# Attention and dense layers in one kernel: row totals placed after the value step, their reciprocals spread by one matmul instead of two

## The chip, the cores and the metric

One core of a Trainium2 chip. Times are device microseconds (us) of whole executions, medians of fast runs (the record sorts executions into fast and slow ones; none here was slow); every profile shown is of state fast, with a granted TensorE clock of 0.998 to 1.0. TensorE is the matrix engine (PE in the profile, PEld its weight loads), DVE is VectorE, ACT ScalarE, POOL GpSimd.

## The reference, cut to what matters

```python
# 4 batches, 8 heads, 768 positions, 64 columns a head: 32 heads, worked on as 16 pairs
mask = q_bucket[:, :, :, None] == k_bucket[:, :, None, :]      # 6-bit hashes of q and k
scores = np.where(mask, scale * q @ k.T, -1e9)
attn = np.exp(scores - scores.max(-1, keepdims=True))
attn = attn / (np.sum(attn, axis=-1, keepdims=True) + 1e-09)   # needs the row totals
x = attn @ v                                                   # the value step
h = x.transpose(0, 2, 1, 3).reshape(3072, 512) @ w_in          # the dense layers
out = (np.maximum(h, 0) ** 2) @ w_out                          # weights come as float64
```

## The kernel before

Scores are kept transposed (keys on partitions), so a row total is a sum over partitions: DVE adds the exponentials of the six key blocks (`add_up`), a matmul with ones sums over the partitions (`sum_up`), and the reciprocals are brought to the layout of the value product (`spread`). The float64 weights are loaded and converted piece by piece beside the attention (`part_weight`, `round_weight`).

```python
def part_weight(i):                       # every third step
    nc.vector.tensor_scalar(out=power, in0=high, ...)          # L127
    nc.vector.tensor_scalar(out=top, in0=high, ...)            # L131
    nc.gpsimd.tensor_scalar(out=power, ...)                    # L136, then L139
    nc.scalar.activation(out=one, in_=top, func=ACTF.Copy, scale=2.0**-23, bias=1.0)   # L142
def round_weight(i):                      # one step later
    nc.vector.scalar_tensor_tensor(out=power, ...)             # L152
    nc.vector.scalar_tensor_tensor(out=one, ...)               # L156
    nc.gpsimd.tensor_tensor(out=pieces[i][3], in0=one, in1=power.bitcast(FP32), op=ALU.mult)
...
def score(pr, kt):                        # 8 matmuls (12 records) into two double banks, then 2 exponentials
    st = [ps_s.tile([P, 2, 512], FP32, name="st") for _ in range(2)]      # pool of two
    ...
def sum_up(pr):
    tot = bank("tot")
    ...                                   # 4 matmuls (8 records) tot <- ones, totals
    nc.vector.transpose(out=flip, in_=tot[:, 0:HS])
    nc.vector.tensor_scalar(out=once, in0=..., scalar1=S * TINY, ..., op0=ALU.add)
    nc.vector.reciprocal(out=once, in_=once)
    onces[pr] = once, tot
def spread(pr):
    once, tot = onces.pop(pr)
    rec = tot[:, HS:HS + 2 * NB]
    for c in range(2):
        nc.tensor.matmul(out=rec[:, c * NB:(c + 1) * NB], lhsT=picks[:, c], rhs=once, ...)
    nc.vector.transpose(out=recs[pr]..., in_=rec...)
...
for u in range(len(steps) + 2):           # 16 pairs x 6 steps
    add_up(*steps[u - 1]); score(*steps[u])
    done = steps[u - 2]
    if done[1] == SB - 1: spread(done[0])
    ...                                   # transposes or hash bits of the next pair
    if done[1] == SB - 2: sum_up(done[0])
    attend(*done)                         # the value block: 4 matmuls (8 records) xo <- v_nat, e
    if done[1] == SB - 1: normalize(done[0])
    i, r = divmod(u, 3)
    if r == 0: load_weight(i); part_weight(i - 1)
    if r == 1: round_weight(i - 1)
```

## Time and profile before

1076.4 us (median of 6 runs, 1075.9 to 1077.3). The dense layers begin at 408.6 us of the profile and are not touched. The attention part is read block by block: the start of one TensorE block to the start of the next, since ends of matmuls are modelled. "Third" and "sixth" count the score blocks of a pair from its first (key block 0). The pair length is the mean distance of spreads over 12 inner pairs.

| block, inner pairs | us |
|---|---|
| score block without a wait (third) | 1.72 |
| sixth score block | 2.10 |
| value block | 1.44 |
| totals | 1.16 |
| spread | 0.47 |
| whole pair | 24.49 |

### The profile page before, as it was taken

What the parts mean: (1) busy time and instruction counts of PE and PEld (TensorE: products, weight loads), DVE (VectorE), ACT (ScalarE), POOL (GpSimd) and SP (SyncE); (2) the same over time, 40 slices, a digit from 0 to 9 for tenths busy, and PEclk for the clock granted to TensorE, in tenths of its full rate; (3) what the DMA queues carried; (4) which work ended last, traced back from release to release, by engine and by line L of the source; (5) the groups of instructions that cost most, each with busy time, mean ns of one, the idle gap of its engine ahead of it and who ended that gap; (6) DMA issues with size and microseconds to landing.
All of it is one profiled execution on the core that took longest, in us unless ns stands there. A gap on an engine that the chain in (4) does not pass through costs nothing.

```text
span 1075.2 us, 10208 instructions
## 1 busy us (share of the span) xinstructions
PE 1055.7 (98%) x4098; PEld 460.4 (43%) x4098; DVE 424.2 (39%) x577; ACT 286.6 (27%) x457; POOL 116.1 (11%) x114
## 2 busy tenths in 40 slices
PE   6999999999999999999999999999999999999998
PEld 3444444444444434444444444444444444444443
DVE  2888888888888883200242024200210021002100
ACT  4555555555555541100110011101110011001100
POOL 1232323223223230000000000000000000000000
PEclk9999999999999999999999999999999999999999
DMA  8333333333331110000330033000000000000000
GB/s 200 84 84 84 84 85 84 84 90 121 107 101 55 40 40 1 0 10 20 127 117 10 20 122 109 15 18 20 1 0 20 20 1 0 20 20 1 0 20 21
DMA packets 65012, 55.24 MB, mean 51 GB/s; under 512 B 51648, under 2 KB 55744, under 8 KB 64960
## 3 DMA queue, kind: packets, MB, share of 16 engines
q1 hardware_dynamic: 63328, 54.14, 17.3%
q8 instruction: 34, 0.56, 0.2%
q10 hardware_dynamic: 1568, 0.39, 0.2%
q14 instruction: 18, 0.15, 0.0%
q0 software_dynamic: 64, 0.00, 0.0%
HBM read 48.24 MB, written 6.29 MB: 51 GB/s over the span
## 4 chain that ended last, share of the span: by engine, by line
PE 82%; DVE 9%; issue 6%; ACT 2%; DMA 0%; SPq 0%; ACTq 0%
PE hid L492 31%; PE y L509 31%; PE st L302 8%; PE xo L334 7%; DVE total L323 2%; PE tp L242 2%; ACT e L309 2%; PE tot L351 2%; DVE bits L266 2%; DVE x_t L384 1%; DVE one L156 1%; PE tot L370 1%; DVE power L152 1%; DVE power L127 1%; DMA q_nat<-in_q_dram 0%
## 5 line engine op out<-in xcount | busy, mean ns | idle before, releaser
L492 PE MATMUL hid<-x_t,w_in 128*128 128x512 f32 x768 | 330.8, 592 | 0.0
L509 PE MATMUL y<-w_out,gate 128*128 128x512 f32 x768 | 330.6, 592 | 0.0
L500 DVE TENSOR_TENSOR gate<-r 128x512 f32<-128x512 f32 x96 | 66.5, 693 | 508.8 <-ACT r L498 506.8
L509 PEld LDWEIGHTS y<-w_out,gate 128*128 128x128 f32 x768 | 145.9, 190 | 183.7 <-issue 183.4
L492 PEld LDWEIGHTS hid<-x_t,w_in 128*128 128x128 f32 x768 | 145.8, 190 | 183.3 <-issue 183.3
L309 ACT ACTIVATE e<-st 128x768 f32<-128x768 f32 x192 | 144.9, 806 | 108.8 <-PE st L302 108.8
L302 PE MATMUL st<-feat,feat 64*128 64x384 f32 x768 | 158.3, 485 | 0.0
L334 PE MATMUL xo<-e,v_nat 128*64 128x384 f32 (+1 forms) x768 | 146.4, 503 | 0.0
L323 DVE TENSOR_TENSOR total<-total,e 128x768 f32<-128x768 f32 x128 | 145.6, 1186 | 1.5 <-ACT e L309 1.5
L498 ACT ACTIVATE r<-hid 128x512 f32<-128x512 f32 x96 | 57.3, 597 | 277.0 <-PE hid L492 277.0
L514 ACT COPY o<-y 128x512 f32<-128x512 f32 x24 | 14.0, 585 | 315.8 <-PE y L509 315.8
L302 PEld LDWEIGHTS st<-feat,feat 64*128 64x128 f32 x768 | 69.3, 188 | 26.9 <-issue 26.4
L334 PEld LDWEIGHTS xo<-e,v_nat 128*64 128x64 f32 x768 | 46.8, 137 | 73.3 <-issue 73.2
L302 PE MATMUL st<-bits,bits 64*128 64x384 bf16 x384 | 70.7, 327 | 3.6 <-ACT e L309 1.5
L302 PEld LDWEIGHTS <-bits 64*128 64x128 bf16 x384 | 19.8, 93 | 69.9 <-issue 56.2
L323 DVE TENSOR_TENSOR total<-e,e 128x768 f32<-128x768 f32 x32 | 45.3, 1456 | 6.3 <-ACT e L309 6.3
L136 POOL TENSOR_SCALAR power<-power 128x512 uint32<-128x512 uint32 x32 | 22.9, 717 | 180.1 <-DVE power L127 180.1
L142 ACT ACTIVATE one<-one 128x512 f32<-128x512 uint32 x32 | 20.2, 630 | 73.3 <-DVE one L131 73.3
L159 POOL TENSOR_TENSOR w_in<-one,power 128x512 f32<-128x512 f32 x16 | 30.7, 1918 | 56.9 <-DVE one L156 56.9
L159 POOL TENSOR_TENSOR w_out<-one,power 128x512 f32<-128x512 f32 x16 | 30.0, 1876 | 55.9 <-DVE one L156 55.9
L247 ACT COPY feat<-tp 128x384 f32<-128x384 f32 x64 | 31.1, 486 | 5.1 <-PE tp L242 5.1
L139 POOL TENSOR_SCALAR power<-power 128x512 uint32<-128x512 uint32 x32 | 29.1, 910 | 2.6
(66 smaller groups left out, 384.1 us busy)
## 6 DMA issues: line engine op xcount, KB each, us to landing
raw<-in_moe_w_in_dram SPq DMA_DIRECT2D x16, 512.0 KB, 4.5
raw<-in_moe_w_out_dram SPq DMA_DIRECT2D x16, 512.0 KB, 4.0
q_nat<-in_q_dram SPq DMA_DIRECT2D x32, 192.0 KB, 5.1
v_nat<-in_v_dram SPq DMA_DIRECT2D x16, 384.0 KB, 3.4
out_dram<-o SPq DMA_DIRECT2D x24, 256.0 KB, 2.0
raw_qk<-in_q_dram SPq DMA_DIRECT2D x8, 768.0 KB, 4.4
raw_qk<-in_k_dram SPq DMA_DIRECT2D x8, 768.0 KB, 4.3
k_nat<-in_k_dram SPq DMA_DIRECT2D x30, 192.0 KB, 5.2
```

Of the source, the lines that this page charges most:

```text
L136: nc.gpsimd.tensor_scalar(out=power, in0=power, scalar1=1151.0, scalar2=896.0, op0=ALU.min, op1=ALU.max,)
L139: nc.gpsimd.tensor_scalar(out=power, in0=power, scalar1=-896.0, scalar2=2.0**23, op0=ALU.add, op1=ALU.mult,)
L159: nc.gpsimd.tensor_tensor(out=pieces[i][3], in0=one, in1=power.bitcast(FP32), op=ALU.mult)
L247: nc.scalar.copy(out=feat[pr, w][:, r * HS:(r + 1) * HS], in_=tp[:, 0:HS])
L302: nc.tensor.matmul(out=st[h][:, c, 0:HS], lhsT=src[pr, 1][rows, key], rhs=src[pr, 0][rows, cut], start=first, stop=not first,)
L309: nc.scalar.activation(out=e[:, 0:S].rearrange("p (c f) -> p c f", c=2), in_=st[h][:, :, 0:HS], func=ACTF.Exp, scale=scale,)
L323: nc.vector.tensor_tensor(out=totals[pr, h], in0=in0, in1=weights[pr, kt, h][:, 0:S], op=ALU.add)
L334: nc.tensor.matmul(out=xo[h * D:(h + 1) * D, c, 0:n], lhsT=nat[pr][2][:, h, kt * D:(kt + 1) * D], rhs=weights[pr, kt, h][:, c * HS:c * HS ...
L492: nc.tensor.matmul(out=hp, lhsT=w_in[:, ft, ff * P:(ff + 1) * P], rhs=x_t[:, ft, i * NCH:(i + 1) * NCH], start=(ft == 0), stop=(ft == NFT ...
L498: nc.scalar.activation(out=r, in_=hp, func=ACTF.Relu)
L500: nc.vector.tensor_tensor(out=g, in0=r, in1=r, op=ALU.mult)
L509: nc.tensor.matmul(out=y, lhsT=gates[ff][:, n * P:(n + 1) * P], rhs=w_out[:, ff], start=(ff == 0), stop=(ff == NFF - 1),)
```

## The change

Intent: the totals need DVE's last addition, so put the value block, which doesn't, ahead of them; and load one 128-column pattern instead of two, paying with a small product on DVE.

```diff
@@ -174,7 +174,8 @@
     lifts = const.tile([P, 1], FP32, name="lifts")
     pj = const.tile([P, NBITS], FP32, name="pj")
     ones = const.tile([P, 32], FP32, name="ones")
-    picks = const.tile([P, 2, P], FP32, name="picks")
+    picks = const.tile([P, P], FP32, name="picks")
+    which = const.tile([P, 2, HS // 32], FP32, name="which")
     NRING = 8
     ring = [const.tile([P, S + 1], FP32, name=f"e{i}") for i in range(NRING)]
 
@@ -204,11 +205,14 @@
 
 
         for g in range(4):
-            for c in range(2):
-                at = 64 * (g // 2) + 32 * c
-                nc.gpsimd.tensor_copy(
-                    out=picks[:, c, g * 32:(g + 1) * 32], in_=ident[:, at:at + 32]
-                )
+            cut = picks[:, g * 32:(g + 1) * 32]
+            at = 64 * (g // 2)
+            nc.gpsimd.tensor_tensor(
+                out=cut, in0=ident[:, at:at + 32], in1=ident[:, at + 32:at + 64], op=ALU.add
+            )
+        nc.gpsimd.memset(which, 0.0)
+        for g in range(4):
+            nc.gpsimd.memset(which[g * 32:(g + 1) * 32, g % 2], 1.0)
 
 
 
@@ -360,16 +364,20 @@
             scalar1=S * TINY, scalar2=None, op0=ALU.add,
         )
         nc.vector.reciprocal(out=once, in_=once)
-        onces[pr] = once, tot
+        both = p_n.tile([P, 2, NB], FP32, name="both")
+        nc.vector.tensor_tensor(
+            out=both, in0=which,
+            in1=once.rearrange("p (o n) -> p o n", o=1).to_broadcast([P, 2, NB]), op=ALU.mult,
+        )
+        onces[pr] = both, tot
 
     def spread(pr):
 
-        once, tot = onces.pop(pr)
+        both, tot = onces.pop(pr)
         rec = tot[:, HS:HS + 2 * NB]
-        for c in range(2):
-            nc.tensor.matmul(
-                out=rec[:, c * NB:(c + 1) * NB], lhsT=picks[:, c], rhs=once, start=True, stop=True
-            )
+        nc.tensor.matmul(
+            out=rec, lhsT=picks, rhs=both.rearrange("p c n -> p (c n)"), start=True, stop=True
+        )
         recs[pr] = p_n.tile([P, S], FP32, name="recs")
         nc.vector.transpose(
             out=recs[pr].rearrange("p (n f) -> p n f", f=32),
@@ -421,9 +429,9 @@
                 if pr + ahead < NP:
                     f(pr + ahead, *args)
             if done is not None:
+                attend(*done)
                 if done[1] == SB - 2:
                     sum_up(done[0])
-                attend(*done)
                 if done[1] == SB - 1:
                     normalize(done[0])
             i, r = divmod(u, EVERY)
```

## The prediction

> **What bounds the kernel now.** I read the page first, then the matrix engine's rows with shapes kept apart, then the timeline of all engines round the end of a head pair, then that of the last pair.
>
> ```profile
> PE 1055.7 (98%) x4098; PEld 460.4 (43%) x4098; DVE 424.2 (39%) x577; ACT 286.6 (27%) x457; POOL 116.1 (11%) x114
> L370 PE MATMUL tot<-once,picks 128*128 128x12 f32 x64 | 9.8, 264 | 0.0
> ```
>
> TensorE looks saturated from end to end. The two dense layers (from 408.59 us) are untouched and only shift. The change lies in the attention part, 16 pairs of 6 steps; a step is a score block (L302) on TensorE, its exponentials on ScalarE (ACT), additions on VectorE (DVE), and a value block (L334) two steps behind. Because matmul ends are modelled, short waits don't show as idle time: I measure from the start of one block to the start of the next. This is the hand-over from one pair to the next:
>
> ```profile
> 232.77 0.55 PE L242 MATMUL tp<-ident,q_nat 128*128 128x128 f32 x3
> 233.25 1.23 PE L351 MATMUL tot<-total,ones 128*32 128x384 f32 x8
> 234.41 1.51 PE L334 MATMUL xo<-e,v_nat 128*64 128x384 f32 x8
> 234.54 0.58 DVE L356 STREAM_TRANSPOSE flip<-tot 128x384 f32<-128x384 f32 x1 [0.96 <-PE tot L351]
> 235.16 0.17 DVE L358 TENSOR_SCALAR once<-flip 128x12 f32<-128x12 f32 x1
> 235.37 0.23 DVE L362 RECIPROCAL once<-once 128x12 f32<-128x12 f32 x1
> 235.51 0.45 DVE L127 TENSOR_SCALAR power<-raw 128x512 uint32<-128x512 uint32 x1
> 235.86 0.34 PE L302 MATMUL st<-bits,bits 64*128 64x384 bf16 x2
> 235.88 0.41 DVE L131 TENSOR_SCALAR one<-raw 128x512 uint32<-128x512 uint32 x1
> 236.38 0.63 ACT L142 ACTIVATE one<-one 128x512 f32<-128x512 uint32 x1 [1.57 <-DVE one L131]
> 237.57 0.61 PE L370 MATMUL tot<-once,picks 128*128 128x12 f32 x4
> 237.74 1.51 ACT L309 ACTIVATE e<-st 128x768 f32<-128x768 f32 x2 [0.72 <-PE st L302]
> 238.04 0.52 PE L242 MATMUL tp<-ident,k_nat 128*128 128x128 f32 x3
> 238.50 1.51 PE L334 MATMUL xo<-e,v_nat 128*64 128x384 f32 x8
> 239.94 0.34 PE L302 MATMUL st<-bits,bits 64*128 64x384 bf16 x2
> ```
>
> Block costs by differences of starts: totals 234.41-233.25 = 1.16, value block 235.86-234.41 = 1.45, score block 237.57-235.86 = 1.71, spread 238.04-237.57 = 0.47, transposes 0.46. In pair 0 the totals took only 0.89, and in pairs 1 to 13 always 1.16 or 1.17: so **0.27 us of each is a wait** for DVE's last addition. A pair lasts 24.49 us. A second wait hides in the last score block of each pair:
>
> ```profile
> 224.84 0.42 DVE L131 TENSOR_SCALAR one<-raw 128x512 uint32<-128x512 uint32 x1
> 225.35 0.63 ACT L142 ACTIVATE one<-one 128x512 f32<-128x512 uint32 x1 [2.86 <-DVE one L131]
> 225.88 1.49 ACT L309 ACTIVATE e<-st 128x768 f32<-128x768 f32 x2
> 227.03 0.71 PE L302 MATMUL st<-bits,bits 64*128 64x384 bf16 x2
> 229.13 0.55 PE L242 MATMUL tp<-ident,q_nat 128*128 128x128 f32 x3
> ```
>
> This block lasts 229.13-227.03 = 2.10 instead of 1.72. The weight conversion (L142) stands in ACT's queue ahead of the exponentials and gets its input late; the exponentials end at 227.37, and until then the second half of the score banks isn't free. **That costs 0.38 us per pair**, and DVE is its origin: from the normalisation on, DVE works without a gap up to L131.
>
> **What the Trainium skill says.** "TensorE: Matmul & The Clock Gate", LDWEIGHTS: loading weights takes columns/1.2 ns, so 107 ns for 128 columns. The trace agrees: spread is 4 matmul records (an fp32 matmul is two) at 0.47/4 = 0.117 us, though each moves only 12 columns. Same page, Architectural detail: ACT and DVE run strictly first in, first out; the L142 case above shows that on ACT. "VectorE: DVE Perf Modes", The TRN2 errata: an fp32 tensor_tensor takes (N+151)/0.96 ns; the 512-element gate product gives 691 and the page of the profile has 693. The clock page, Part 1: the array runs at half clock after an idle window of about 3.4 us; see the tail below.
>
> **The change part by part.** T is the start of the score block that follows the hand-over.
>
> 1. Totals after the value block: the matmuls are the same, but DVE's additions have 1.45 us more, so the wait of 0.27 goes. Saving 0.27 per pair.
> 2. Spread with one matmul: two weight loads instead of four, 0.47 to about 0.235. Twelve more columns add some 0.01 per record, by the score block's rate (feature matmuls of 384 columns, two side by side, take 0.32: four records in 0.65). Saving 0.23 per pair.
> 3. Added on DVE: one product of 128x24. Estimate from the skill's formula (24+151)/0.96 = 182 ns, and 35 ns between dependent instructions (235.16-234.54-0.58 = 0.04), so 0.22 us.
> 4. What moves: today the transpose starts 0.13 after the totals block ended, i.e. 1.32 before T. Afterwards the totals end at T, so it starts at T+0.13: the chain is **1.45 later against the score block**. In today's spacing: once +0.62, reciprocal +0.83, product +1.09, done +1.28, i.e. T+1.41. Spread comes at T+1.72: it just makes it, with 0.3 to spare.
> 5. The weight step follows on DVE: L131 at today's +1.34 after the transpose plus 0.22, so T+1.69 (today T+0.02). On ACT, L131's start to the end of both exponentials is 227.37-224.84 = 2.53 where the conversion leads. So exponentials end at T+4.22 instead of T+3.39. The next score block wants their banks at T + 1.72 + 0.235 + 0.46 + 1.44 = T+3.86. **A new wait of 0.36, with 0.04 to the restart 0.40 us**, in the third score block of the next pair.
> 6. The normalisation comes before this new wait, and DVE's unbroken work starts from it, so the older wait is measured from there too. TensorE arrives 0.40 later, and the old 0.38 vanishes. The two don't add: per pair the larger counts.
>
> Sum for an inner pair: -0.27 -0.23 +0.40 -0.38 = -0.48, times 13 = 6.2 us. The first hand-over has no wait to lose: -0.23+0.40-0.38 = -0.2. At the last but one the totals took 1.65, so -0.76-0.23 = -1.0; the new wait is harmless there, as the last pair hangs on DVE's additions.
>
> The tail:
>
> ```profile
> 401.88 2.23 PE L351 MATMUL tot<-total,ones 128*32 128x384 f32 x8 [1.94 <-DVE total L323]
> 404.04 2.63 PE L334 MATMUL xo<-e,v_nat 128*64 128x384 f32 x8
> ```
>
> Here TensorE idles 1.94, then runs the value block in 2.56 (404.04 to 406.60) instead of 1.44, a half clock. Afterwards this block runs inside that gap, at full clock; but after the totals TensorE must wait out the chain of 1.28 before spread, and may then be slow in the last value block. Dense layers start at 408.59 today; I estimate 406.6 if the clock holds, 408.5 if not: -1.0.
>
> Total 6.2+0.2+1.0+1.0 = 8.4: 1076.4-8.4 = 1068.0. I choose 1068.5, since step 5 is more likely to come out dearer than cheaper.
>
> **The rivals.**
> A. *No new wait*: ACT gets its conversion early enough. Then the old 0.38 stays and a pair takes 23.99, nearly the same as mine: about 1068. For it: a margin of 0.69 between the exponentials' end and the next score block today. Against it: the shift is 0.83.
> B. *The new wait is larger and eats the gain*: the product takes 0.4 instead of 0.22, or the exponentials come behind yet another ACT instruction. Each 0.1 us costs 1.5 us in all; a wait of 0.8 gives about 1074.5. For it: DVE additions beside GpSimd's products run at 1.45 instead of 0.93, so DVE durations do stretch here; against it: GpSimd is idle in this stretch.
> C. *Spread itself waits*: the margin of 0.3 is lost, TensorE stops in order. Beyond it each 0.1 again costs 1.5 us; 1070 to 1073. Against it: nothing stands between transpose and product on DVE.
> D. *Nothing lost at all*: both waits gone, 0.88 per pair, 1062. Against it: the queue order of ACT.
>
> **Range and chances.** Mine and A fall together at 1067 to 1069; B and C spread upward, the tail is worth 1 either way. Range 1065.5 to 1072.5. A result beyond 2% would need 1.35 us per pair, which no part carries: faster 0.01, same 0.98, slower 0.01.
>
> **What would show it.** Totals at 0.89 each; spread at 0.23 to 0.25 with 32 records instead of 64; the product near 0.18; the conversion L142 starting about T+2.2; the third score block of a pair (the one after the transposes and value block that follow spread) at about 2.1 instead of 1.72, and the sixth back at 1.72; pair length near 24.0. I am wrong if the pair takes over 24.3 (B or C, told apart by which block is long) or under 23.8 (D).

## The result, and the profile after

The changed kernel takes **1066.93 us** (median of 6, 1065.64 to 1067.32) against 1076.38; the ratio is 0.991, interval 0.9897 to 0.9923. (A ratio here is the mean time of one kernel's fast runs over that of the other's of the same rounds, so not quite the ratio of the medians.) This is faster by 0.9%, so within the 2% called the same, and inside the predicted range.

The timeline of all engines at the same hand-over, after:

```profile
231.57 0.85 PE L355 MATMUL tot<-total,ones 128*32 128x384 f32 x8
232.36 0.34 PE L306 MATMUL st<-bits,bits 64*128 64x384 bf16 x2
232.49 0.58 DVE L360 STREAM_TRANSPOSE flip<-tot 128x384 f32<-128x384 f32 x1 [2.03 <-PE tot L355]
...
233.58 0.18 DVE L368 TENSOR_TENSOR both<-which,once 128x24 f32<-128x24 f32 x1
...
234.02 0.42 DVE L131 TENSOR_SCALAR one<-raw 128x512 uint32<-128x512 uint32 x1
234.08 0.40 PE L378 MATMUL tot<-both,picks 128*128 128x24 f32 x2
...
234.32 0.52 PE L246 MATMUL tp<-ident,k_nat 128*128 128x128 f32 x3
...
234.53 0.63 ACT L142 ACTIVATE one<-one 128x512 f32<-128x512 uint32 x1 [2.83 <-DVE one L131]
...
235.07 1.49 ACT L313 ACTIVATE e<-st 128x768 f32<-128x768 f32 x2
236.22 0.71 PE L306 MATMUL st<-bits,bits 64*128 64x384 bf16 x2
...
238.31 0.55 PE L246 MATMUL tp<-ident,k_nat 128*128 128x128 f32 x3
```

T is 232.36. Totals 232.36-231.57 = 0.79; spread 234.32-234.08 = 0.24; the product ends at T+1.40 and spread starts at T+1.72; the conversion starts at T+2.17, the exponentials end at 236.56 = T+4.20, and the third score block lasts 238.31-236.22 = 2.09. In its place the sixth score block now lasts 1.73. A pair takes 23.90.

The timeline of TensorE at the end of the last pair:

```profile
393.95 1.72 PE L355 MATMUL tot<-total,ones 128*32 128x384 f32 x8
397.06 0.40 PE L378 MATMUL tot<-both,picks 128*128 128x24 f32 x2 [1.38 <-DVE both L368]
397.39 1.51 PE L338 MATMUL xo<-e,v_nat 128*64 128x384 f32 x8
```

TensorE stops 1.38 ahead of spread, as foreseen; the last value block keeps its full rate (1.44 to the dense layers at 398.83). There is no half clock in the tail of this profile.

That is not the change's doing alone. The profile before shows the half clock from 402.93 to 406.34, but not every execution had it. The four profiles with a half clock in the tail have a mean granted clock of 0.998, the eight without it 0.999 or 1.0. Of the 25 executions of the kernel before that ran beside the experiments, 11 show 0.997 or 0.998 (median 1077.2 us) and 14 show 1.0 (median 1076.2): so in most of them, by this reading, the tail kept its rate, which is worth 1.0 us. The six executions of the changed kernel all show 0.999, but the half clock can come back under the new order: e7 (below) stops only a little longer, and its last value block takes 2.46. Its timeline of TensorE, with the clock at 0.5 from 399.24 to 402.65:

```profile
398.56 0.40 PE L380 MATMUL tot<-twice,picks 128*128 128x24 f32 x2 [1.60 <-DVE twice L373]
398.89 2.53 PE L338 MATMUL xo<-e,v_nat 128*64 128x384 f32 x8
```

**Where the 9.8 us of the two profiles lie** (dense layers begin at 408.59 and 398.83), by shifts of the spreads: 0.10 up to the first spread of the attention part, 13 pair lengths shorter by 0.59 each, 7.71 in all, then 1.28 to the last but one hand-over's end, 2.03 from there to the dense layers: 11.12. Against it stands 1.36 at the start: the first value block begins at 23.71 instead of 22.35. The start isn't a matter of the step studied. TensorE runs at half rate until the full clock is granted: a matmul record of the hash projections takes 0.84 before that and 0.48 after it. The trace marks the grant at 12.90 in this profile and at 10.40 in the one before, so the second hash projection took 1.50 instead of 0.81 (the load that TensorE's first instruction waits for also landed 0.3 later). In the twelve profiles the grant comes between 9.8 and 12.9 and the first value block between 22.0 and 24.1. The four latest grants (12.2 to 12.9) belong to the four latest starts (23.2 to 24.1), and one of these four, e8, has the old constants; four kernels with the new constants had early grants (10.1 to 10.8) and early starts (22.1 to 22.6). So the 1.36 follows the moment of the grant, which varies from execution to execution; whether the new constants make late grants more frequent was not isolated.

### The profile page after: what moved, and what is told of

The parts are those of the page before. It is cut to its first block, busy times and chain, and to the rows that moved or that the text cites. A ratio compares the mean times of both kernels' runs of the same rounds, so it can differ in the third digit from the quotient of the medians.

```text
span 1065.4 us, 10162 instructions
## 1 busy us (share of the span) xinstructions
PE 1046.3 (98%) x4066; PEld 456.0 (43%) x4066; DVE 426.7 (40%) x593; ACT 285.0 (27%) x457; POOL 116.2 (11%) x115
## 4 chain that ended last, share of the span: by engine, by line
PE 93%; DVE 3%; ACT 3%; issue 1%; DMA 1%; SPq 0%; ACTq 0%
PE hid L500 31%; PE y L517 31%; PE st L306 13%; PE xo L338 11%; ACT e L313 2%; PE tp L246 2%; PE near L263 2%; PE tot L355 1%; DVE flip L360 1%; DMA q_nat<-in_q_dram 1%; DVE one L131 0%; DVE power L127 0%; DVE once L366 0%; PE st L263 0%; DVE once L362 0%
```

## The experiments

Ten kernels, all results correct but one. The pair is the mean over 12 inner pairs, the blocks are medians over inner pairs of each kernel's timeline; "before" ran beside each at 1076.3 to 1077.1.

| run | us (runs) | ratio to before, interval | pair | totals | spread | third | sixth |
|---|---|---|---|---|---|---|---|
| before | 1076.4 | - | 24.49 | 1.16 | 0.47 | 1.72 | 2.10 |
| after | 1066.9 (6) | 0.9910, 0.9897-0.9923 | 23.90 | 0.78 | 0.24 | 2.09 | 1.73 |
| e1 order only | 1069.7 (5) | 0.9937, 0.9924-0.9951 | 24.11 | 0.79 | 0.47 | 1.72 | 2.10 |
| e2 spread only | 1074.3 (5) | 0.9979, 0.9966-0.9993 | 24.27 | 1.16 | 0.24 | 1.72 | 2.10 |
| e3 weight step first | 1067.6 (5) | 0.9916, 0.9902-0.9929 | 23.89 | 0.78 | 0.24 | 1.72 | 2.10 |
| e4 mid conversion later | 1067.5 (4) | 0.9904, 0.9889-0.9919 | 23.88 | 0.79 | 0.24 | 2.09 | 1.72 |
| e5 both conversions later | 1061.9 (4) | 0.9868, 0.9853-0.9883 | 23.51 | 0.79 | 0.24 | 1.72 | 1.72 |
| e6 before, both later | 1069.4 (5) | 0.9925, 0.9912-0.9939 | 24.29 | 0.79 or 1.89 | 0.47 | 1.72 | 1.72 |
| e7 product twice | 1070.4 (5) | 0.9938, 0.9924-0.9951 | 24.10 | 0.78 | 0.24 | 2.31 | 1.72 |
| e8 before, rounding later | 1067.2 (4) | 0.9905, 0.9890-0.9920 | 23.98 | 1.04 | 0.47 | 1.72 | 1.72 |
| e9 before, no rounding | 1062.8 (4) | 0.9877, 0.9860-0.9893 | 23.73 | 0.78 | 0.47 | 1.72 | 1.72 |
| e10 product four times | 1077.3 (4) | 1.0012, 0.9995-1.0028 | 24.53 | 0.79 | 0.24 | 2.35 | 1.72 |

**e1 and e2: each part alone.** e1 is the changed kernel with the two spread matmuls, their two patterns and no product; e2 is it with the old order:

```diff
+                if done[1] == SB - 2:       # e2
+                    sum_up(done[0])
                 attend(*done)
-                if done[1] == SB - 2:
-                    sum_up(done[0])
```

> Only the order: totals after the value block, spread still with two matmuls and no product. My theory: the totals block costs 0.79 us as after the change (today 1.16), and without the product the weight conversion comes 0.26 earlier than after the change while spread still lasts 0.47, so the exponentials end at about T+3.94 and the next score block wants its banks at T+4.09: no new wait in the third score block, and the old wait of 0.38 in the sixth stays. Pair length 24.49 - 0.37 = 24.12 us, some 1070 us in all. Rival (the order alone makes a new wait that eats its gain): pair length 24.3 or more, 1073 us or more.

> Only the spread: one matmul of 24 columns and the product, totals before the value block as in the kernel before. My theory: spread 0.24 instead of 0.47 us; the product delays the exponentials by 0.26, less than their margin of 0.69, so no new wait; the wait in the totals block and the old wait in the sixth score block stay. Pair length 24.49 - 0.23 = 24.26, some 1072.8 us in all. Rival (the loop hangs on VectorE, so a product more there costs what spread gains): pair length 24.4 to 24.5, 1075 to 1076 us.

Both pair lengths came as foreseen: 24.11 and 24.27. The order is worth 0.38, the spread 0.23 per pair; together 0.61, and the change has 0.59. In time e1 fits (1069.7), e2 came at 1074.3, 1.5 us above the expectation, though its profile (dense layers at 405.27) shows 3.3 us gained. Four of its five executions show a clock of 0.997 or 0.998; the fifth, with 1.0, took 1072.8 as expected. Neither rival holds: neither pair length is in its range.

**e3, e4, e5: the two waits of the score blocks.** e3 issues the weight step ahead of `sum_up`; e4 and e5 give ACT's conversion its own call, one step later. Both also move the rounding one step later, so they differ from each other by the hand-over's conversion alone:

```diff
 attend(*done)                                        # e3
+if r == 0: load_weight(i); part_weight(i - 1)
 if done[1] == SB - 2: sum_up(done[0])
 if done[1] == SB - 1: normalize(done[0])
-if r == 0: load_weight(i); part_weight(i - 1)
```

```diff
-        nc.scalar.activation(out=one, in_=top, ...)   # e5, in part_weight; e4 keeps it there where u % 6 == 0
+if r == 1: convert_weight(i - 1)                      # the same activation, behind this step's exponentials
-if r == 1: round_weight(i - 1)
+if r == 2: round_weight(i - 1)                        # e4 and e5
```

> The changed kernel with the two VectorE instructions of the weight step issued ahead of the totals' chain, so ScalarE gets its conversion early and the new wait in the third score block must go. My theory (the larger of the two waits counts): the old wait of about 0.37 returns in the sixth score block, pair length 23.9 as after the change, 1066 to 1068 us. Rival (the new wait is a cost by itself that adds up): pair length 23.53, some 1061.5 us.

> The changed kernel with only the mid-pair weight conversion (the one that stood behind the old wait) one step later; the one at the hand-over stays where it is. The mirror image of the run that took away only the new wait. My theory (the larger of the two counts): the third score block still lasts 2.10, the sixth 1.72 as after the change, pair length 23.90, 1066 to 1068 us, nothing gained. Rival (each conversion moved is worth its share of the 5 us that moving both gave): 1064 to 1065 us.

> The changed kernel with every weight conversion of ScalarE one step later, behind that step's exponentials (and the rounding two steps after the load instead of one). My theory: neither the third nor the sixth score block waits any more, all score blocks last 1.72, pair length 23.53, 14 pairs by 0.37 = 5.2 us less than the changed kernel: some 1061.7 us. Rival (VectorE's unbroken work is the bound of the pair, TensorE's waits only mirror it): the totals or another block takes up the wait, pair length stays 23.9, 1067 us.

In e3 the third score block lost its wait, and the sixth got the old one back; its timeline of TensorE:

```profile
223.48 0.72 PE L306 MATMUL st<-bits,bits 64*128 64x384 bf16 x2
...
225.58 0.55 PE L246 MATMUL tp<-ident,q_nat 128*128 128x128 f32 x3
```

That block is 225.58-223.48 = 2.10, and the pair is no shorter. e4 is the mirror: the cause of the old wait taken away, nothing gained (1067.5, rival 1064 to 1065). Only e5, both at once, gains:

```profile
229.88 1.51 ACT L323 ACTIVATE e<-st 128x768 f32<-128x768 f32 x2 [2.48 <-PE st L316]
...
231.64 0.65 ACT L151 ACTIVATE one<-one 128x512 f32<-128x512 uint32 x1
...
231.92 0.34 PE L316 MATMUL st<-bits,bits 64*128 64x384 bf16 x2
...
233.64 0.55 PE L256 MATMUL tp<-ident,k_nat 128*128 128x128 f32 x3
```

The exponentials (229.88 to 231.39) now lead, the conversion follows in ACT's free time, and the third score block lasts 1.72. The pair is 23.51, 5.1 us are gained over the change. e5 is the best correct kernel: **1061.9 us**, 1.3% under the kernel before, its interval clear of that of the change. A wait that costs nothing by itself (e3, e4) was worth 0.39 per pair together with the other: the larger of the two counts, because both are measured from the same normalisation.

**e7 and e10: the product's place in the chain.**

```diff
+        twice = p_n.tile([P, 2, NB], FP32, name="twice")          # e10: three such in a row
+        nc.vector.tensor_tensor(out=twice, in0=which, in1=both, op=ALU.mult)
-        onces[pr] = both, tot
+        onces[pr] = twice, tot
```

> The changed kernel with a second product of 128x24 behind the first (a copy by the same 0 and 1 pattern, so results stay right). My theory: the chain and the weight conversion come 0.22 later, the new wait grows from 0.37 to 0.6 (third score block 2.32), spread still just in time at 0.24; pair length 24.12, 14 pairs by 0.22 = 3.1 us more than the changed kernel: some 1070 us. Rival (VectorE is idle there anyway, so an instruction more costs nothing): 1067 us.

> The changed kernel with three more products in a row behind the first (results stay right): it uses up the margin of spread. My theory: the chain ends 0.66 later, at T+2.06, so spread starts at T+2.1 instead of T+1.72 and the score block ahead of it seems 0.4 longer; the third score block waits as well, 0.37 + 0.66 - 0.4 = 0.6; pair length 23.90 + 0.66 = 24.56, 14 pairs by 0.66 = 9 us more than the changed kernel, some 1076 us: all the gain gone. Rival (spread's wait and the third block's wait add in full, 0.4 + 0.66): pair length 24.9, 1081 us.

e7's third score block (timeline of TensorE) is 238.57-236.25 = 2.32, and its second matmul waits for the exponentials:

```profile
236.25 0.33 PE L306 MATMUL st<-bits,bits 64*128 64x384 bf16 x1
236.86 0.32 PE L306 MATMUL st<-bits,bits 64*128 64x384 bf16 x1 [0.28 <-ACT e L313]
...
238.57 0.55 PE L246 MATMUL tp<-ident,k_nat 128*128 128x128 f32 x3
```

So an instruction of 0.18 on DVE, an engine idle for 2.03 just before, costs 0.20 per pair and 3.5 us in all. (Three of its five executions show a clock of 0.998, like the profile with the half clock in its tail; the other two took 1069.9 and 1070.0, so about 3.0 without the half clock.) e10 uses up spread's margin; the timeline of TensorE has it at 238.15, against a score block that began at 236.04:

```profile
238.15 0.40 PE L382 MATMUL tot<-more,picks 128*128 128x24 f32 x2 [0.33 <-DVE more L374]
```

T+2.11, as foreseen (T+2.1). The pair is 24.53, the time 1077.3: the whole gain is gone. The rival's 24.9 is not reached; spread's wait shortens the wait behind it.

**e6: the same edit on the kernel before.** As e5, on the kernel before.

> The kernel before with every weight conversion one step later, the same edit that gave 5 us on the changed kernel. My theory: before the change VectorE's unbroken work from the normalisation to the last addition sets the arrival of the totals; the sixth score block falls to 1.72, but the totals block waits 0.38 longer (1.54 instead of 1.16), pair length stays 24.49, 1075 to 1077 us. Rival (the wait of 0.38 was a cost by itself): pair length 24.11, some 1071 us.

This expectation fell. The time is 1069.4 (1067.4 to 1072.7), nearer the rival's 1071. The profiled execution is the slowest of the five (1072.7; the other four took 1067.4 to 1069.8), so its mean pair of 24.29 and what follows hold for that execution; how the pairs split in the faster ones was not profiled. Its timeline shows why neither expectation is right. Two pairs in turn, DVE and GpSimd, then the totals and the value block:

```profile
229.20 2.89 DVE L333 TENSOR_TENSOR total<-total,e 128x768 f32<-128x768 f32 x2
229.36 1.91 POOL L169 TENSOR_TENSOR w_out<-one,power 128x512 f32<-128x512 f32 x1 [4.01 <-DVE one L166]
231.03 0.83 PE L361 MATMUL tot<-total,ones 128*32 128x384 f32 x2
...
232.92 1.51 PE L344 MATMUL xo<-e,v_nat 128*64 128x384 f32 x8
```

```profile
253.11 1.81 DVE L333 TENSOR_TENSOR total<-total,e 128x768 f32<-128x768 f32 x2
253.26 2.78 POOL L169 TENSOR_TENSOR w_out<-one,power 128x512 f32<-128x512 f32 x1 [3.91 <-DVE one L166]
...
255.86 0.85 PE L361 MATMUL tot<-total,ones 128*32 128x384 f32 x8
256.65 1.51 PE L344 MATMUL xo<-e,v_nat 128*64 128x384 f32 x8
```

The same two additions take 2.89 beside a GpSimd product of 1.91, or 1.81 beside one of 2.78: one of the two engines is held up, and which one alternates here from pair to pair. The single instructions show where the choice falls: the first addition takes 0.95 or 0.94 in both pairs, and the product ends 1.13 after the end of the first addition in one pair (the second addition then takes 2.02) and 1.13 after the end of the second in the other (the second takes 0.94). So what alternates is whether the product or the second addition goes first once the first addition is done. The stretch on DVE from normalisation to last addition is 18.4 in one kind of pair and 16.4 in the other, where it is 18.0 in nearly all pairs of the kernel before. In the first kind the totals wait until they take 1.89, in the second they don't wait and take 0.79. My theory took the stretch of 18.0 as fixed; it isn't, as soon as instructions move.

**e8 and e9: the same stretch, shortened.** e8 moves the rounding out of part of it, e9 leaves it out (wrong results).

```diff
 if r == 0:
-    load_weight(i); part_weight(i - 1)
+    part_weight(i - 1); round_weight(i - 2); load_weight(i)     # e8
-if r == 1: round_weight(i - 1)
```

```diff
-        nc.vector.scalar_tensor_tensor(out=power, ...)            # e9, both in round_weight
-        nc.vector.scalar_tensor_tensor(out=one, ...)
```

> The kernel before, order and spread untouched, with the rounding of a weight piece (two VectorE instructions, 1.27 us) moved from the steps between normalisation and last addition to behind the conversion two steps later, so at the hand-over, where VectorE waits anyway. My theory: VectorE's last addition and its mid-pair conversion come early enough, so the totals block falls to its length without a wait, and the sixth score block to 1.72: pair length 23.74 to 23.84, 1066 to 1067.5 us, as much as the change gains. It also settles the totals' own cost in the old place: 0.79 if the 0.89 of pair 0 held a wait of 0.10, 0.89 if the place before the value block is dearer. Rival (the gain needs the new order): 1074 to 1076 us.

> The kernel before without the two VectorE instructions that round a weight piece; results are wrong on purpose. It asks the loop question cleanly, since the earlier trial (conversions moved on the kernel before) changed how VectorE and GpSimd overlap. My theory: the pair of the kernel before is set by VectorE's stretch of 18.0 us from the normalisation to the last addition; shortened by some 2.5 us it leaves no wait: totals block 0.79 in the old place (so 0.37 of its 1.16 was a wait, not 0.27), sixth score block 1.72, pair length 24.49 - 0.37 - 0.38 = 23.74, some 1066 us. Rival (the old place of the totals is dearer by itself): totals block 0.89 or more, pair length 23.85 or more.

e8 reaches the change's time with neither of its edits (1067.2), so the gain doesn't need the new order. But its pair is 23.98 where I had 23.74 to 23.84, because the stretch fell only to 17.5: the two rounding instructions left in it now run beside GpSimd and take 1.10 and 1.26 instead of 0.68 each, and DVE, now early, waits 1.53 for TensorE's hash matmuls. The totals still wait (1.04), so it didn't settle their own cost. The 0.51 per pair is some 6.6 us; most of the rest lies at the end, where it needs 20.95 us from the last but one hand-over to the dense layers, and the kernel before 24.07. e9 does; its timeline of TensorE:

```profile
227.12 0.85 PE L344 MATMUL tot<-total,ones 128*32 128x384 f32 x8
227.90 1.51 PE L327 MATMUL xo<-e,v_nat 128*64 128x384 f32 x8
```

In the old place, without a wait, the totals take 0.78; the sixth score block is 1.72, the pair 23.73 as foreseen (23.74). The stretch fell to 16.1, so by 1.9 and not by the 2.5 expected, which was enough. The time of 1062.8 is below the expected 1066; like e8 it needs 20.95 us instead of 24.07 from the last but one hand-over to the dense layers, where the kernel before hangs on DVE.

## Why the prediction was right, point by point

- **Totals (step 1)**: mechanism right, size off. I took 0.27 for the wait, because pair 0 with 0.89 seemed free of it. It wasn't: its last addition ends at 37.62 (four additions, start 32.99, 4.63 long) and the value block follows at 38.46, 0.84 later, and in the waiting pairs that distance is 0.83 too. Free of a wait they take 0.78 or 0.79, in the new place (after, e1) and in the old (e9). The wait was 0.38, and this is the term that makes a pair 0.59 shorter instead of 0.48: 13 times 0.11 = 1.4 us.
- **Spread (step 2)**: predicted 0.235, measured 0.24; e2 has it alone, 0.23 per pair.
- **Product and its place (steps 3 and 4)**: 0.182 estimated, 0.182 measured; end at T+1.41, measured T+1.40. The margin of 0.3 ahead of spread is real: e7's product fits in, e10's three don't.
- **New wait (step 5)**: 0.40 predicted, 0.38 measured, from the conversion ahead of the exponentials in ACT's queue. e3 gives the conversion its input earlier, e5 puts it behind the exponentials, and in both the wait goes; e7 shows that it grows with the chain.
- **The larger counts (step 6)**: shown by e3, e4 and e5 together. This was rival A's answer too: without the new wait the old one would have stayed, with the same pair length.
- **Last hand-over**: -1.0 predicted, -1.28 measured in the interval that ends it.
- **Tail**: -1.0 predicted as the middle of two cases; the case "clock holds" (406.6) came true, 2.0 us in the profiles. Part of this is luck: about 1 us of it is the half clock of the profiled execution before, which most executions of that kernel (14 of 25) did not show.
- **Sum**: 8.4 predicted and 7.9 chosen; the attention part gave 11.1, the start took back 1.4 in the profile, by the late grant of the full clock. That the total of 9.4 lies near the prediction is partly luck, these two errors against each other.
- **Rivals**: B (a larger wait) and C (spread waits) didn't occur, e7 and e10 show what they would have cost: 3.5 us for 0.22 and 10.4 us for 0.66. (B's 1.45 for an addition beside GpSimd is a mean: the trace has 32 of one kind with a mean of 1.456, and each takes 0.95 or 2.03.) D (nothing lost) isn't this change but e5.
- **What stays open**: why DVE gives way to GpSimd in one pair and not in the next; what decides whether a stop of TensorE in the tail brings the half clock; and whether the new constants make a late grant at the start more frequent.

## What to carry to other kernels

Before moving a block on the busy engine, list what hangs on it in the queues of the idle engines: here an idle DVE and an idle ACT turned 0.22 us of extra work and 1.45 us of lateness into a new wait of TensorE, because a conversion nobody was in a hurry for stood ahead of the exponentials. Two waits in one loop that are measured from the same event don't add; removing one may show nothing until the other goes too, so try them together before dropping the idea. And don't take the shortest case seen for a case without a wait: check the distance from the event that would release it. Before crediting a change with a faster start or tail, look at the granted clock of every execution and not of the profiled one alone: here it moved the start by 1.4 us and the tail by 1.0.

## What the Trainium skill lacked or had wrong

- "TensorE: Matmul & The Clock Gate", Part 1: it puts the return to half clock after an idle window of about 3.4 us. Of shorter stops it only says, for another kernel, that frequent short idle times between groups of matmuls can do it, without a length. Here half clocks of 3.41 each followed single stops of TensorE of 1.94 (before), 2.95 (e2), 1.60 (e7) and 2.04 (e10), and in the 3.4 us ahead of it TensorE was busy for 1.42 in the kernel before and 1.80 in e7. But e3 kept its full rate after stops of 1.73 and 1.51, so the length of the stop alone doesn't decide. In every profile all changes of the clock lie whole multiples of 3.413 us apart (before: 392.53 is 115 of them), but e3's stop of 1.73 lies whole inside one such step (391.10 to 394.51), so its place among the steps doesn't decide alone either.
- Same page, LDWEIGHTS: the 107 ns for 128 columns are near what a record of these fp32 patterns costs (0.47/4 and 0.24/2, so 0.12 us), but the page doesn't say that an fp32 matmul appears as two records, each with its own load: the spread of 24 columns cost 0.24, of two times 12 columns 0.47.
- "VectorE: DVE Perf Modes", The TRN2 errata: (N+151)/0.96 holds far below the sizes that it names: 182 ns for 24 columns, measured 182 to 184.
- "SBUF — State Buffer", Who interferes with whom: "Issue order, not op shape, decides who blocks." The trace agrees that one of the two is held up (additions 2.89 beside a product of 1.91, or 1.81 beside 2.78), but the product starts 0.15 to 0.17 after the additions in both kinds, so the order of these starts doesn't tell which engine is held up. In the second kind the second addition started 0.71 after the product and was done first all the same; the page has nothing finer.
